# Attention steps 255 to 414 of a two-layer kernel: fixed strings of 16 steps, more double runs of values, five score tiles copied out by VectorE, ten tiles of exponentials

## The chip, the core and the metric

One core of a Trainium2 chip runs the whole program. TensorE multiplies (PE in the profile; its weight loads are PEld), VectorE is DVE, ScalarE ACT, GpSimd POOL, and SyncE (SP) issues most of the loads. Compute engines work on SBUF; TensorE writes its results to PSUM, which has eight banks of 512 float32 a partition. Each engine takes its instructions strictly in order and waits on semaphores for what the others make. The metric is the device time of one execution in microseconds.

## The reference

Four residual layers follow each other: attention, a Fourier mixing, attention, Fourier mixing. This is cut to the attention, which the change touches (S = 2048 tokens, D = 640, H = 32 heads of Dh = 20):

```python
qkv = (x @ wqkv).reshape(B, S, 3, H, Dh).transpose(2, 0, 3, 1, 4)
q, k, v = qkv[0], qkv[1], qkv[2]
scores = jnp.einsum("bhqd,bhkd->bhqk", q, k) * (Dh ** -0.5)
p = softmax(scores, axis=-1)
o = jnp.einsum("bhqk,bhkd->bhqd", p, v)
return o.transpose(0, 2, 1, 3).reshape(B, S, D) @ wo
```

## The kernel before

The 32 heads are taken in 8 groups of four, the queries in 4 blocks of 512, the keys in 16 blocks of 128. A **step** is one triple of them, in that order, so that a layer has 8 x 4 x 16 = 512 steps, and 16 steps in a row share one accumulator. A step makes two **score tiles** of 128 keys x (2 heads x 512 queries): `scores(n, j)` (line 606) issues two matmuls into a PSUM tile `psc` of two banks and one exponential on ScalarE (line 616) that reads `psc` and writes a tile `e` in SBUF. There are three `psc` tiles, taken in turn (six banks), and seven `e` tiles. `values(n)` (line 618) multiplies both `e` tiles of a step with the value matrix into the accumulator `acc` (one bank; line 624: four matmuls in the program, which the chip's records show as eight). One bank is left (`fill`).

After the 16th step of a head group's block, `finish` (line 629) copies `acc` away by a transpose on VectorE (line 631), normalizes it in six more VectorE instructions (lines 633 to 641) and sends eight DMAs from GpSimd's queue (line 645). The next step's values need `acc` free, so they wait for that transpose alone.

Three kinds of other work are laid between the steps. **Fills** are pieces of the projections for later heads: five matmuls of `pqk` (line 106) into the `fill` bank. After three pieces VectorE takes the product from the bank (`keep`, lines 91, 94, 262 to 267), and a **norm** follows (`norms`, line 283: one matmul, and a VectorE reduction at line 284). **Compares** are VectorE work on tables that GpSimd loads, to test that the Fourier matrices have the expected symmetry (pairs of lines 918 and 914, and smaller ones); `compare(n)` issues up to two of them a step. **Bounds** (lines 528 to 540) are small VectorE instructions with one power on GpSimd (line 536) between their head (528 to 530) and their tail (538, 540).

The order is that of the code, in `sweep` (line 648): each engine gets its instructions in the order in which Python issues them. In steps 255 to 414 no written string rules before the change: each step makes two score tiles, then a fill where `due` says so (three in 16 steps), or else one or two steps of values. This gives, on TensorE, two score tiles, then values of one step (a single run) or two (a double run), and so on. Strings written out by letters (`plan`, line 748) rule parts of the steps before 236 and those from 448.

Of the kernel before, what the change touches and what calls it, by code (L numbers as in the profile page):

```python
# [5 lines left out]
F32 = mybir.dt.float32  # L6
# [3 lines left out]
AF = mybir.ActivationFunctionType  # L10
# [6 lines left out]
SCALE = DH ** -0.5  # L17
# [25 lines left out]
def mha_fnet_kernel(ctx, tc, x_in, wqk, wv, wo, seq, hid, nat_seq, nat_hid, out):  # L43
    nc = tc.nc
    V, A, G, PE = nc.vector, nc.scalar, nc.gpsimd, nc.tensor
# [100 lines left out]
    class Qkv:  # L146
# [29 lines left out]
        def norm(s, k, tiles=range(2)):  # L176
            for i in tiles:
                normed(s.xn[k][:, i], s.xn[k][:, i], s.rs[k], i)
# [369 lines left out]

    class Attention:
        THIN = 236  # L550

        def __init__(s, qkv, L):
            s.a = qkv
            s.k, s.q, s.e = {}, {}, {}
            s.o = dr.tile([2, D, S], F32, name=f"o_{L}")
            s.steps = [(g, qb, kc) for g in range(H // 4) for qb in range(NB) for kc in range(NT)]

# [46 lines left out]
            G.memset(z[:H].bitcast(F32), 0.0)  # L604
            nc.sync.dma_start(s.a.shift["b"][:, 1], z[:H].bitcast(F32))

        def scores(s, n, j):

            g, qb, kc = s.steps[n]
            p = bank(f"p{(2 * n + j) % 3}", [128, 2, 512], "psc")  # L610
            for i in range(2):
                r = slice(64 * i, 64 * i + 62)
                PE.matmul(p[:, i], s.k[g, kc // 8, j][r, kc % 8 * 128:(kc % 8 + 1) * 128], s.q[g, qb, j][r],  # L613
                          start=True, stop=True)
            e = s.e[n, j] = s.room(f"e{(2 * n + j) % 7}", [2, 512], F32, "e")
            A.activation(e, p, AF.Exp, scale=SCALE)  # L616

        def values(s, n):
            g, qb, kc = s.steps[n]
# [9 lines left out]
        def finish(s, g, qb):  # L629
            t0 = s.room("ofsh", [16, 32], F32, "of")  # L630
            V.transpose(t0.rearrange("p b c -> p (b c)"), s.acc)  # L631
            rc = const.tile([128, 16], F32, name="rc", bufs=2)
            V.tensor_scalar(rc, t0[:, :, DH], 1e-30, None, op0=OP.max)
            V.reciprocal(rc, rc)
            t1 = s.room("on", [16, 32], F32, "on")
            V.tensor_tensor(t1, t0, rc[:, :, None].to_broadcast([128, 16, 32]), op=OP.mult)
            t2 = s.room("ofsh", [512], F32, "ot")
            V.transpose(t2, t1.rearrange("p b c -> p (b c)"))
            hl = [s.room("on", [512], F32R, "oh").bitcast(F32), t2]
            V.tensor_copy(hl[0].bitcast(F32R), t2)  # L640
            V.tensor_tensor(t2, t2, hl[0], op=OP.subtract)
            for k in range(2):
                for j in range(4):
                    h = 4 * g + j
                    G.dma_start(s.o[k, h * DH:(h + 1) * DH, qb * 512:(qb + 1) * 512],  # L645
                                hl[k][32 * j:32 * j + DH])

        def sweep(s, shift, begin, fill=lambda n: None, plan=None, block=None, compare=lambda n: None):
            done = calm = n = 0

            def opened(n):
                g, qb, kc = s.steps[n]
                begin(n, g, qb, kc)
                last = qb == NB - 1
                if kc == (7 if last else 10 if g in LATE else 4) and not (last and g == H // 4 - 1):
                    s.qload(*((g, qb + 1) if not last else (g + 1, 0)), shift)
                if last and g + 1 < H // 4:
                    for f, j in {1: [(0, 0)], 9: [(0, 1)], 11: [(1, 0)]}.get(kc, []):
                        s.kload(g + 1, f, j)
                if qb == 0 and kc == 0 and g:  # L660
                    s.kload(g, 1, 1)

            while n < len(s.steps):
                opened(n)
                order = plan and plan(n)
                if order:

                    while done < n - 1:
                        s.values(done)
                        done += 1  # L670
                    t = 2 * n
                    for c in order:
                        if c == "s":
                            m, j = divmod(t, 2)
                            if not j and m > n:
                                opened(m)
                            s.scores(m, j)
                            if j:
                                compare(m)
                            t += 1  # L680
                        elif c == "v":
                            s.values(done)
                            done += 1
                        else:
                            (block if c == "f" else fill)(t // 2)
                    n = t // 2
                    continue
                s.scores(n, 0)
                s.scores(n, 1)
                more, owed = fill(n) and n >= 2 and n + 1 < len(s.steps), n - 1 - done  # L690
                compare(n)
                n += 1
                if plan and n <= s.THIN:
                    count = owed + 1
                elif more and owed < 3:
                    calm = n + 1
                    continue
                else:
                    count = min(owed, 1)
                    if owed > 1 and (done + 1) % NT and n > calm:  # L700
                        calm = n + 1
                        count = 2
                for _ in range(count):
                    s.values(done)
                    done += 1
            for n in range(done, len(s.steps)):
                s.values(n)

        def run(s, done, project, check):

            work, tasks, later = s.a.work(), s.a.vweights(1, s.a.fill, pause=[lambda: None] * 2), list(check)
# [3 lines left out]
            tail, n = {}, 448  # L715
# [22 lines left out]
            def fill(n):  # L738
# [4 lines left out]
                elif s.work and n >= max(s.rest, s.THIN) and due(n + 1):  # L743
                    block(n)
                    s.rest = max(s.rest, n + 2)
                    return s.work and not s.a.silent

            def plan(n):
                if n in tail:
                    return tail[n]  # L750
                if s.blocks >= 58 or s.after:
                    return
                whole = 32 <= s.blocks < 48
                if n % 4 == 1 and n + (4 if whole else 8) < s.THIN and (whole or s.blocks % 2 == 0):
                    return "sssfsssvvssvv" if whole else "sssfsssvvssvvsssfssvvsssnvv"

            def compare(n):


                if n < 8:  # L760
                    return
                for _ in range(2):
                    if not later or n < s.landed or (len(check) - len(later)) * 490 >= n * len(check):
                        break
                    task = later.pop(0)
                    if isinstance(task, tuple):
                        s.landed = n + 5
                        task = task[1]
                    task()
# [8 lines left out]
            def begin(n, g, qb, kc):  # L778


                if qb == NB - 1 and g + 1 < H // 4:
                    when, to = 0, g + 1
                    c0, c1 = to * 80 // 128, ((to + 1) * 80 - 1) // 128
                    keys = [c0, (c1, 0) if to in LATE else c1, ND + c0, ND + c1] + (["v"] if to >= 4 else [])
                else:
                    when, to, keys = 5, g, [(((g + 1) * 80 - 1) // 128, qb + 1)]
                if to != g or g in LATE and qb < NB - 1:
                    if kc == when:
                        need(n, *keys)
                        s.shift = s.a.bound(to, s.room)  # L790
                    if kc - when in (0, 3, 5):
                        next(s.shift)

                if tasks and n % 2 == 0 and n >= 16 and n % 64 < 54:
                    tasks.pop(0)()
                for f in project.early.get(n, []):
                    f()

            s.sweep("b", begin, fill, plan, block, compare)
            assert not s.work and not later and not tasks and not project.parts, (len(later), len(tasks))  # L800

        def general(s, done, project):
# [252 lines left out]
    class Project:  # L1055
# [100 lines left out]
        @staticmethod  # L1156
        def scaled(dst, g, r, b2, b):

            A.activation(dst[:, :HD + 1], g[:, :HD + 1], AF.Identity, scale=r, bias=b2)
            A.activation(dst[:, 0:HD + 1:HD], g[:, 0:HD + 1:HD], AF.Identity, scale=r, bias=b)  # L1160
            A.activation(dst[:, HD + 1:], g[:, HD + 1:], AF.Identity, scale=r, bias=zero[:dst.shape[0]])
# [393 lines left out]
    tasks = check.tasks()  # L1555
    cut = next(i for i, t in enumerate(tasks) if 2 * i >= len(tasks) and isinstance(t, tuple))
    tasks = (tasks[:cut], tasks[cut:])
# [202 lines left out]
```

## Time and profile before

| | |
|---|---|
| three runs | 2429.83 us median (2429.36 to 2431.03) |
| the profiled execution | 2429.18 us, its span 2427.4 us |
| granted TensorE clock, mean | 0.998 |
| exponentials, line 616 | x2048, 1918.1 us busy, 1060 ns of one |
| value matmuls, line 624 | x8192, 1030.0 us busy |
| score matmuls, line 613 | x4096, 744.0 us busy |

A row of a group reads: line, engine, operation, output<-input by the program's names, partitions x elements, count, then busy time, mean of one, and the idle time of that engine before it with what ended it. A row of the timeline reads: start and length in us, engine, line, operation, output<-input, count of instructions merged; in square brackets the engine's idle time before, and what ended it. Matmuls overlap, so their run's cost is read from the start of one run to the start of the next. A row of the windows gives, for a stretch, busy time (and instructions) of PE, PEld, DVE, ACT and POOL in this order, then the granted clock, the share of the DMA engines and GB/s. The first layer's steps 255 to 414 lie between about 611 and 914.5 us, the second layer's between about 1815 and 2119 us.

### The profile page before, as it was taken

Reading aid. Unit: us, or ns where it says so; the run is one execution under the profiler, and the core shown is the slowest. Engines: PE = TensorE matmul, PEld = TensorE weight load, DVE = VectorE, ACT = ScalarE, POOL = GpSimd, SP = SyncE. Lnnn points to the kernel's source line nnn. Section 1 sums busy time; section 2 is a strip of 40 time slices with the busy share of each in tenths; the row PEclk is TensorE's granted clock in tenths of the full one; section 3 lists DMA queues with packets and bytes.
Section 4 is the critical chain, followed back from the end, with each engine's and each line's share of the span. In section 5 each row is a group of like instructions: output and inputs, shape, how many; then the busy total and the mean of one; then the engine's idle time right before and its main releaser. Section 6 shows DMA issues by size and latency. Waiting matters only on the chain. (4 is left out here: it accounts for less than half of the span.)

```text
span 2427.4 us, 43836 instructions
## 1 busy us (share of the span) xinstructions
PE 2406.3 (99%) x16200; PEld 1155.5 (48%) x16200; DVE 1012.3 (42%) x2328; ACT 2099.7 (86%) x2402; POOL 552.3 (23%) x1080
## 2 busy tenths in 40 slices
PE   9999999999999999999999999999999999999998
PEld 8544444543333332339885444454433333333496
DVE  7333432234333434427773444332433333334275
ACT  5799998899999999994357999988999999999852
POOL 3122221012222212114341212211111212113143
PEclk9999999999999999999999999999999999999999
DMA  6334341123232325419663232322231322152195
GB/s 213 130 122 137 110 150 59 60 69 119 80 93 89 105 72 159 124 48 320 238 230 116 96 118 89 116 65 77 77 109 57 96 59 81 52 154 78 53 333 211
DMA packets 136702, 289.01 MB, mean 119 GB/s; under 512 B 31628, under 2 KB 56108, under 8 KB 136480
## 3 DMA queue, kind: packets, MB, share of 16 engines
q1 hardware_dynamic: 93408, 171.07, 21.7%
q0 software_dynamic: 43072, 115.06, 14.8%
q8 instruction: 130, 2.13, 0.4%
q14 instruction: 92, 0.75, 0.1%
HBM read 187.38 MB, written 92.70 MB: 115 GB/s over the span
## 5 line engine op out<-in xcount | busy, mean ns | idle before, releaser
L616 ACT ACTIVATE e<-psc 128x1024 f32<-128x1024 f32 x2048 | 1918.1, 1060 | 106.5 <-PE psc L613 96.4
L624 PE MATMUL acc<-e,v 128*32 128x512 f32 x8192 | 1030.0, 600 | 0.4 <-DVE of L631 0.4
L613 PE MATMUL psc<-stq,stk 62*128 62x512 f32 x4096 | 744.0, 446 | 3.1 <-ACT e L616 2.2
L613 PEld LDWEIGHTS psc<-stq,stk 62*128 62x128 f32 x4096 | 335.0, 184 | 699.9 <-ACT e L616 545.5
L624 PEld LDWEIGHTS acc<-e,v 128*32 128x32 f32 x8192 | 210.7, 109 | 410.0 <-issue 378.0
L106 PE MATMUL pqk<-xt,wqk 128*128 128x512 f32 x1200 | 320.9, 408 | 2.1 <-ACT xt L93 1.1
L645 POOL DMA_DIRECT2D o<-oh x256 | 131.6, 522 | 784.6 <-DVE oh L640 737.0
L91 DVE CAST hl<-pqk 128x512 fp32r<-128x512 f32 x64 | 44.3, 692 | 587.7 <-PE pqk L106 587.7
L106 PEld LDWEIGHTS pqk<-xt,wqk 128*128 128x128 f32 x1200 | 214.2, 189 | 86.1 <-issue 38.4
L106 PE MATMUL pv<-wv,xt 128*128 128x320 f32 x960 | 151.7, 314 | 0.0
L106 PEld LDWEIGHTS pv<-wv,xt 128*128 128x128 f32 x960 | 141.0, 188 | 13.5 <-issue 10.2
L631 DVE STREAM_TRANSPOSE of<-acc 128x512 f32<-128x512 f32 x64 | 45.8, 715 | 208.7 <-PE acc L624 208.7
L645 POOL DMA_DIRECT2D o<-ot x256 | 128.2, 508 | 1.8 <-DVE xr L1118 0.6
L275 POOL DMA_DIRECT2D scrk<-hl x40 | 27.9, 697 | 377.4 <-DVE hl L94 266.6
L275 POOL DMA_DIRECT2D scrq<-hl x40 | 28.4, 711 | 352.8 <-DVE hl L94 293.2
L99 PE MATMUL py<-wo,o 128*128 128x320 f32 x320 | 101.2, 316 | 0.0
L914 DVE TENSOR_REDUCE far<-cq 128x1 f32<-128x512 f32 (+5 forms) x169 | 98.5, 584 | 5.7
L101 PE MATMUL py<-wo,o 128*128 128x320 f32 x320 | 98.9, 309 | 0.0
L100 PE MATMUL py<-wo,o 128*128 128x320 f32 x320 | 98.8, 309 | 0.0
L918 DVE TENSOR_TENSOR cq<-cq 128x512 f32<-128x512 f32 (+4 forms) x166 | 96.5, 581 | 1.2 <-DMA cq<-in_nat_seq_dram 1.2
L314 DVE COPY v<-pv 128x320 f32<-128x320 f32 x32 | 15.7, 489 | 161.8 <-PE pv L106 161.8
L284 DVE TENSOR_REDUCE top<-pn 32x1 f32<-32x512 f32 x50 | 33.7, 676 | 72.3 <-PE pn L283 72.2
(219 smaller groups left out, 1744.5 us busy)
## 6 DMA issues: line engine op xcount, KB each, us to landing
cq<-in_nat_seq_dram POOLq DMA_DIRECT2D x64, 512.0 KB, 5.3
scrq<-hl POOLq DMA_DIRECT2D x40, 512.0 KB, 4.1
scrk<-hl POOLq DMA_DIRECT2D x40, 512.0 KB, 3.2
stq<-scrq SPq DMA_DIRECT2D x256, 80.0 KB
stk<-scrk SPq DMA_DIRECT2D x128, 160.0 KB
chl<-matrix SPq DMA_DIRECT2D x32, 512.0 KB
o<-o SPq DMA_DIRECT2D x32, 384.0 KB
stq<-scrq SPq DMA_DIRECT2D x256, 40.0 KB
```

What stands on the lines that cost most here:

```text
L99: PE.matmul(out_ap, ah, bh, start=start, stop=False)
L100: PE.matmul(out_ap, ah, bl, start=False, stop=False)
L101: PE.matmul(out_ap, al, bh, start=False, stop=stop)
L106: yield lambda i=i, j=j, k=k: PE.matmul(out_ap, a[i], b[j], start=dc == 0 and k == 0, stop=dc == ND - 1 and k == 2)
L275: G.dma_start(s.scr["qk"[k]][c * 128:(c + 1) * 128, :, tb * 512:(tb + 1) * 512], hl.bitcast(F32))
L613: PE.matmul(p[:, i], s.k[g, kc // 8, j][r, kc % 8 * 128:(kc % 8 + 1) * 128], s.q[g, qb, j][r], start=True, stop=True)
L616: A.activation(e, p, AF.Exp, scale=SCALE)
L624: PE.matmul(s.acc[32 * j:32 * j + 32], s.a.v[kc][:, v0:v0 + 32], s.e[n, j // 2][:, j % 2], start=kc == 0, stop=kc == NT - 1, skip_group_ch ...
L631: V.transpose(t0.rearrange("p b c -> p (b c)"), s.acc)
L645: G.dma_start(s.o[k, h * DH:(h + 1) * DH, qb * 512:(qb + 1) * 512], hl[k][32 * j:32 * j + DH])
L914: V.tensor_reduce(to, x, op=OP.max, axis=AX.X, apply_absolute_value=True)
L918: V.tensor_tensor(y, x, y, op=op)
```

## The change

Steps 255 to 414 (ten strings of 16 in each layer) follow one written string. Its letters: `s` a score tile with its exponential out of PSUM; `d` a score tile that VectorE first copies from `psc` to its `e` tile, after which the exponential works in place in SBUF; `v` the values of the oldest step that has none yet; `f` a fill; `n` the norm, if one is pending. Two more tiles of score lead over values are let in (`done < n - 2`).

Between the value runs, the string is: `ss f s v`, `ss v` four times, `sd f ssd vv`, `ssd vv`, `ssd f ss vv`, `ss v n`, `ss vv`, `ssd vv`, and one `s` that joins the next string's first two. Its first value is that of the 15th step of a group's 16, so that its third `v` closes a group and its fourth opens the next.

Three more `e` tiles come from the space of a weight tile that is no longer used (`widen`), and are given back after step 414 (`narrow`). The part of `finish` behind the transpose, the compares, and the tasks that load later weights are no longer issued where they arise, but put into `held`; `release` issues them after the letter at hand, unless one of the next two letters is a `d`. This holds in all steps, with and without a string.

```diff
     class Attention:
         THIN = 236
+        LOOSE = range(255, 415, 16)
+        STRING = "ssfsvssvssvssvssvsdfssdvvssdvvssdfssvvssvnssvvssdvvs"
...
+            s.ring = [lambda k=k: s.room(f"e{k}", [2, 512], F32, "e") for k in range(7)]
...
-        def scores(s, n, j):
+        def scores(s, n, j, copied=False):
...
-            e = s.e[n, j] = s.room(f"e{(2 * n + j) % 7}", [2, 512], F32, "e")
-            A.activation(e, p, AF.Exp, scale=SCALE)
+            s.ring.append(s.ring.pop(0))
+            e = s.e[n, j] = s.ring[-1]()
+            if copied:
+                V.tensor_copy(e, p)
+            A.activation(e, e if copied else p, AF.Exp, scale=SCALE)
+
+        def widen(s):
+            x = s.a.fill("wv", [3, 2, 512], F32, "ex")
+            s.extra = [lambda k=k: x[:, k] for k in range(3)]
+            s.ring = s.extra + s.ring
+
+        def narrow(s):
+            s.ring = [f for f in s.ring if f not in s.extra]
...
             V.transpose(t0.rearrange("p b c -> p (b c)"), s.acc)
+            s.held.append(lambda: s.scaled(t0, g, qb))
+
+        def scaled(s, t0, g, qb):
             rc = const.tile([128, 16], F32, name="rc", bufs=2)
...
+            def release():
+                while s.held:
+                    s.held.pop(0)()
...
-                    while done < n - 1:
+                    while done < n - (2 if n in s.LOOSE else 1):
                         s.values(done)
                         done += 1
+                    if n in s.LOOSE and done == n - 1:
+                        order = order.replace("v", "", 1)
                     t = 2 * n
-                    for c in order:
-                        if c == "s":
+                    for k, c in enumerate(order):
+                        if c in "sd":
...
-                            s.scores(m, j)
+                            s.scores(m, j, c == "d")
                             if j:
-                                compare(m)
+                                s.held.append(lambda m=m: compare(m))
...
-                            (block if c == "f" else fill)(t // 2)
+                            (block if c == "f" else fill if n < s.THIN else norm)(t // 2)
+                        if k + 1 < len(order) and "d" not in order[k + 1:k + 3]:
+                            release()
...
+                release()
                 s.scores(n, 0)
...
+            def norm(n):
+                if s.after:
+                    f, s.after = s.after[1], None
+                    f()
...
+                if n in s.LOOSE:
+                    if n == s.LOOSE[0]:
+                        s.widen()
+                    return s.STRING
+                if n == s.LOOSE[-1] + 16:
+                    s.narrow()
...
-                    tasks.pop(0)()
+                    s.held.append(tasks.pop(0))
```

What this moves is seen in the program's order, engine by engine. First TensorE, in the first layer, around steps 306 to 312 (`psc` scores, `acc` values, `pqk` a fill; `ex` are the three new exponential tiles; values of one step are four rows here). Before:

```order
L613 MATMUL psc<-stq,stk 128x512 x4
L106 MATMUL pqk<-xt,wqk 128x512 x5
L613 MATMUL psc<-stq,stk 128x512 x4
L624 MATMUL acc<-e,v 32x512 x4
L613 MATMUL psc<-stq,stk 128x512 x4
L624 MATMUL acc<-e,v 32x512 x8
L613 MATMUL psc<-stq,stk 128x512 x4
L624 MATMUL acc<-e,v 32x512 x4
```

And now, from the run that ends in the string's first copied tile:

```order
L616 MATMUL psc<-stq,stk 128x512 x4
L106 MATMUL pqk<-xt,wqk 128x512 x5
L616 MATMUL psc<-stq,stk 128x512 x6
L638 MATMUL acc<-ex,v 32x512 x2
L638 MATMUL acc<-e,v 32x512 x6
L616 MATMUL psc<-stq,stk 128x512 x6
L638 MATMUL acc<-e,v 32x512 x8
```

Score tiles now come three at a time (x6) where two steps of values follow (eight rows), instead of two at a time with mostly one step of values.

Second, VectorE in the same place, from the transpose that frees the accumulator on. Before:

```order
L631 STREAM_TRANSPOSE of<-acc 128x512
L633 TENSOR_SCALAR rc<-of 128x16
L634 RECIPROCAL rc<-rc 128x16
L636 TENSOR_TENSOR on<-of,rc 128x512
L638 STREAM_TRANSPOSE ot<-on 128x512
L640 CAST oh<-ot 128x512
L641 TENSOR_TENSOR ot<-ot,oh 128x512
L918 TENSOR_TENSOR cq<-cq 128x512
L914 TENSOR_REDUCE far<-cq 128x1
L538 TENSOR_SCALAR bound<-bound 32x1
L540 CAST sh<-bound 32x64
```

And now:

```order
L645 STREAM_TRANSPOSE of<-acc 128x512
L650 TENSOR_SCALAR rc<-of 128x16
L651 RECIPROCAL rc<-rc 128x16
L653 TENSOR_TENSOR on<-of,rc 128x512
L655 STREAM_TRANSPOSE ot<-on 128x512
L657 CAST oh<-ot 128x512
L658 TENSOR_TENSOR ot<-ot,oh 128x512
L956 TENSOR_TENSOR cq<-cq 128x512
L952 TENSOR_REDUCE far<-cq 128x1
L538 TENSOR_SCALAR bound<-bound 32x1
L540 CAST sh<-bound 32x64
L621 COPY e<-psc 128x1024
```

The sequence is the same, and the copy of the string's first `d` tile stands behind all of it. In the other strings the same seven instructions of the finish come first; between them and the copy stand, in the first layer's ten strings in order, a compare pair and the bound's head; the same; the head; pair and tail (the rows above); a maximum with eight small compare instructions; nothing; nothing; pair and tail; pair and head; a maximum and the head. In the second layer: the head; three small ones and the head; the head; tail and pair; a pair; nothing; a maximum with two small ones; the tail; the head; the head.

More of the change, by code (lines that the diff above doesn't have):

```diff
@@ L550, in mha_fnet_kernel @@
         THIN = 236
+        LOOSE = range(255, 415, 16)
+        STRING = "ssfsvssvssvssvssvsdfssdvvssdvvssdfssvvssvnssvvssdvvs"
         def __init__(s, qkv, L):
             s.a = qkv
-            s.k, s.q, s.e = {}, {}, {}
+            s.k, s.q, s.e, s.held = {}, {}, {}, []
+            s.ring = [lambda k=k: s.room(f"e{k}", [2, 512], F32, "e") for k in range(7)]
             s.o = dr.tile([2, D, S], F32, name=f"o_{L}")
@@ L646, in finish, with sweep @@
                                 hl[k][32 * j:32 * j + DH])
-        def sweep(s, shift, begin, fill=lambda n: None, plan=None, block=None, compare=lambda n: None):
+        def sweep(s, shift, begin, fill=lambda n: None, plan=None, block=None, compare=lambda n: None, norm=None):
             done = calm = n = 0
+            def release():
+                while s.held:
+                    s.held.pop(0)()
             def opened(n):
@@ L707, in sweep @@
                 s.values(n)
+            release()
         def run(s, done, project, check):
@@ L794, in begin @@
                 if tasks and n % 2 == 0 and n >= 16 and n % 64 < 54:
-                    tasks.pop(0)()
+                    s.held.append(tasks.pop(0))
                 for f in project.early.get(n, []):
                     f()
-            s.sweep("b", begin, fill, plan, block, compare)
+            s.sweep("b", begin, fill, plan, block, compare, norm)
             assert not s.work and not later and not tasks and not project.parts, (len(later), len(tasks))
```

## The prediction

> **What bounds the kernel now.** I read the page's busy shares first, then busy time by windows, then TensorE's timeline in the stretch that is changed (first layer; the second layer's rows look alike).
>
> ```profile
> PE 2406.3 (99%) x16200; PEld 1155.5 (48%) x16200; DVE 1012.3 (42%) x2328; ACT 2099.7 (86%) x2402; POOL 552.3 (23%) x1080
> ...
> core 0: us, PE busy (x) PEld busy (x) DVE busy (x) ACT busy (x) POOL busy (x), PEclk, DMA share, GB/s
> 611.00:914.50 303.50, 303.50 (x2080) 107.36 (x2076) 117.55 (x262) 299.46 (x320) 62.87 (x113) 1.00 0.28 88
> 914.50:943.40 28.90, 28.73 (x195) 8.54 (x194) 12.76 (x32) 28.90 (x33) 6.72 (x12) 1.00 0.37 110
> ```
>
> Steps 255 to 414 last 303.5 us for 160 steps: TensorE without a gap, ScalarE at 98.7%, granted clock 1.00, VectorE at 39%. Two engines are nearly full. One period of 16 steps on TensorE shows which is the tighter:
>
> ```profile
> 699.43 0.73 PE L613 MATMUL psc<-stq,stk 62*128 62x512 f32 x4
> 700.10 1.06 PE L624 MATMUL acc<-e,v 128*32 128x512 f32 x8
> 701.10 0.73 PE L613 MATMUL psc<-stq,stk 62*128 62x512 f32 x4
> ...
> 703.41 1.06 PE L624 MATMUL acc<-e,v 128*32 128x512 f32 x8
> 704.41 0.90 PE L613 MATMUL psc<-stq,stk 62*128 62x512 f32 x4
> 705.24 1.43 PE L106 MATMUL pqk<-xt,wqk 128*128 128x512 f32 x5
> 706.59 0.73 PE L613 MATMUL psc<-stq,stk 62*128 62x512 f32 x4
> ...
> 708.25 0.73 PE L613 MATMUL psc<-stq,stk 62*128 62x512 f32 x4
> 708.91 1.92 PE L624 MATMUL acc<-e,v 128*32 128x512 f32 x16
> 710.77 0.73 PE L613 MATMUL psc<-stq,stk 62*128 62x512 f32 x4
> ...
> 729.80 0.73 PE L613 MATMUL psc<-stq,stk 62*128 62x512 f32 x4
> ...
> 821.63 1.07 PE L624 MATMUL acc<-e,v 128*32 128x512 f32 x8
> 822.51 0.38 PE L283 MATMUL pn<-sq,ind 128*32 128x512 bf16 x1
> 822.82 0.73 PE L613 MATMUL psc<-stq,stk 62*128 62x512 f32 x4
> ```
>
> From start to next start: a score run of two tiles 0.66 (708.25 to 708.91), a run of values 1.00, a double run 1.86, a fill 1.35, a norm 0.19 more (821.63 to 822.82 is 1.19). Sixteen steps hold 16 score runs, 10 single and 3 double value runs, 3 fills and a norm: 10.56 + 10.0 + 5.58 + 4.05 + 0.19 = 30.4; the trace has 30.37 (699.43 to 729.80). So TensorE sets the pace. ScalarE's own floor stands where it never waits:
>
> ```profile
> 914.53 29.45 ACT L616 ACTIVATE e<-psc 128x1024 f32<-128x1024 f32 x32
> ...
> 973.52 1.02 ACT L616 ACTIVATE e<-psc 128x1024 f32<-128x1024 f32 x1 [0.21 <-PE psc L613]
> ```
>
> (29.45 - 1.02) / 31 = 0.917 a tile, 29.34 for a period. ScalarE idles 1.03 of 30.37.
>
> **What is removed.** The new string has 14 score runs and 11 value runs (6 single, 5 double) for the same 32 tiles, 16 steps, 3 fills and norm.
>
> ```profile
> 972.90 0.97 PE L613 MATMUL psc<-stq,stk 62*128 62x512 f32 x6
> ...
> 1066.22 0.97 PE L613 MATMUL psc<-stq,stk 62*128 62x512 f32 x6
> 1067.13 1.92 PE L624 MATMUL acc<-e,v 128*32 128x512 f32 x16
> ```
>
> Three tiles take 0.91, two 0.66: about 0.24 a tile and 0.18 a run. Scores: 14 x 0.18 + 32 x 0.24 = 10.20, 0.36 less. Values: 6 x 1.00 + 5 x 1.86 = 15.3, 0.28 less. TensorE alone would need 29.73. That is 0.39 over ScalarE's floor, so from here each wait of ScalarE counts.
>
> **What is late next.** A first score tile's exponential starts 0.62 after its run (972.90 to 973.52). ScalarE's stock is the work it has beyond what TensorE has just delivered; it idles where this runs out. A single run with two tiles takes 1.66 and brings 1.83 of ScalarE's work, +0.18. "ss vv" takes 2.52 for 1.83: -0.68. "sss vv" (2.76 for 2.75), the first piece and "ssvn" come out even; both pieces with a fill and a double (0.66 + 1.35 + 0.91 + 1.86 = 4.78 for five tiles, 4.59) lose 0.19. The stock is zero at the first of the four "ssv", grows to 0.70, and loses 0.28 at the border of a head group: there the old string put a fill between the last values of one group and the first of the next, now only two score tiles stand there. Let the last values start at T. VectorE's transpose of the accumulator starts at T + 1.14 (703.41 to 704.55, below), which is 0.08 after the values end (704.47); I take that 0.08 for every signal from engine to engine. It ends at T + 1.86, so TensorE, back at T + 1.66, goes on at T + 1.94: 0.28. The remaining 0.42 goes into the pieces with fills, and the later "ss vv" finds none: ScalarE idles 0.68 there, about 0.12 a little before (TensorE itself waits for score buffers in the second piece with a fill), and 0.16 at the first copied tile (next part). 29.34 + 0.96 = 30.30 a string, 0.07 under 30.37: 1.4 us for 20 strings is all that is left of 20 x 0.64.
>
> **The copies.** No row copies 128x1024 out of PSUM; the nearest are
>
> ```profile
> L91 DVE CAST hl<-pqk 128x512 fp32r<-128x512 f32 x64 | 44.3, 692 | 587.7 <-PE pqk L106 587.7
> ...
> L640 DVE CAST oh<-ot 128x512 fp32r<-128x512 f32 x64 | 27.3, 427 | 2.2
> ...
> L314 DVE COPY v<-pv 128x320 f32<-128x320 f32 x32 | 15.7, 489 | 161.8 <-PE pv L106 161.8
> ```
>
> 1.06 ns an element between the two PSUM rows (pqk and pv) gives 1.23 us. Bounds: two casts out of PSUM, 1.38, and two out of SBUF, 0.85. I take 1.23, the line through the PSUM rows. When may the first of the five begin? In program order it stands behind the whole finish of the head group:
>
> ```profile
> 704.55 0.72 DVE L631 STREAM_TRANSPOSE of<-acc 128x512 f32<-128x512 f32 x1 [4.99 <-PE acc L624]
> ...
> 707.73 0.69 DVE L641 TENSOR_TENSOR ot<-ot,oh 128x512 f32<-128x512 f32 x1
> 708.34 0.68 DVE L918 TENSOR_TENSOR cq<-cq 128x512 f32<-128x512 f32 x1
> 709.06 0.69 DVE L914 TENSOR_REDUCE far<-cq 128x1 f32<-128x512 f32 x1
> 709.66 0.13 DVE L538 TENSOR_SCALAR bound<-bound 32x1 f32<-32x1 f32 x1
> 709.83 0.25 DVE L540 CAST sh<-bound 32x64 fp32r<-32x64 f32 x1
> 709.94 0.67 DVE L918 TENSOR_TENSOR cq<-cq 128x512 f32<-128x512 f32 x1
> ...
> 823.65 0.18 DVE L528 TENSOR_REDUCE boundm<-top 32x10 f32<-32x40 f32 x1
> ...
> 824.05 0.15 DVE L530 TENSOR_TENSOR bound<-bound 32x1 f32<-32x1 f32 x1
> ```
>
> The finish takes 704.55 to 708.34, 3.79, so VectorE is free at T + 1.14 + 3.79 = T + 4.93. The tile is there at T + 1.00 + 0.66 + 0.28 + 1.00 + 0.66 + 1.00 (its run starts, T + 4.60) + 0.73 + 0.08 = T + 5.41, so 0.48 is spare. ScalarE wants it at T + 4.60 + 0.62 + 0.42 of stock + 0.92 for the tile before it = T + 6.56; copied at once it comes at 5.41 + 1.23 + 0.08 = T + 6.72. So VectorE work beyond the spare 0.48 is ScalarE's idle time, one for one. TensorE cannot work ahead meanwhile: three score buffers block it. The change holds VectorE work back only when a copy is one or two letters away, and these items are issued earlier. Extra work ahead of the first copy, by the new program order: a compare pair (1.32, 708.34 to 709.66) and the bound's head (about 0.5, 823.65 to past 824.05), late by 1.34: 3 strings; the pair and the bound's tail (0.28), 1.12: 3; the pair alone, 0.84: 1; other compare work, which I estimate at 0.6 late, between none and the longest: 4; head or tail alone, within the spare time: 6; nothing: 3. Sum 4.0 + 3.4 + 0.8 + 2.4 = 10.6 us. The other four copies have VectorE free, or 0.5 to spare on ScalarE.
>
> Exponentials now read SBUF five times a string.
>
> ```profile
> L93 ACT ACTIVATE xt<-xs 128x512 fp32r<-128x512 f32 x20 | 10.8, 618 | 3.4 <-DMA scrk<-hl 3.2 <-DMA stk<-scrk 0.2
> ...
> L93 ACT ACTIVATE xt<-ptr 128x512 fp32r<-128x512 f32 x20 | 10.2, 605 | 0.7 <-PE ptr L187 0.7
> ```
>
> The same copy costs 13 ns more from SBUF: 100 exponentials, 1.3 us. The Trainium skill ("VectorE: DVE Perf Modes", section "The TRN2 errata — SBUF-src ops pay a fixed extra latency per instruction") has 224 fixed cycles for ScalarE from SBUF and 172 from PSUM at 1.2 GHz, a rule against this change; by it an estimate of 43 ns each, 4.3 us, and a time 3 us higher. The rows' 13 ns speak for less.
>
> **At no cost.** Ten exponential tiles in place of seven only remove waits. Holding the finish and the compares elsewhere moves VectorE work by a step: before step 255 TensorE has no gap, after 414 VectorE is busy 12.76 of 28.90. Were that cover gone, only the transpose could be waited for, and it isn't held.
>
> **The sum.** The profiled execution took 2429.18 (span 2427.4; median 2429.83): - 1.4 + 10.6 + 1.3 gives 2439.7.
>
> **Rivals.** (1) *VectorE is in time*: the compare items wait elsewhere, or TensorE reaches the first copied tile over a microsecond later than I count. Strings of 30.30, - 1.4 + 1.3: 2429.1, no change. For it: VectorE is idle 61% of the stretch. Against: the finish and the pair stand in one row ahead of the copy. (2) *Faster*: ScalarE holds one more tile (0.92) at the first copied tile, the point from which it decides; the delays then vanish and so do its idle spells, and TensorE's 29.73 + 0.28 rules. 20 x 0.36 less: 2422.0. For it: ten exponential tiles and early-freed buffers let TensorE lead. Against: three score buffers bound the lead, and only tiles already copied are free of that. (3) *Worse*: the bound's tail on VectorE waits for GpSimd's power, which stands behind eight output DMAs of 0.52 (4.1 us), issued after the finish; they end about T + 9, and the third copy is wanted at T + 10.2. If the finish slips by 1.5 it costs up to 1 us in eight strings: 2447.7. That the change does not do what it says is ruled out by the program order, which has the runs and the copies.
>
> ```profile
> L645 POOL DMA_DIRECT2D o<-oh x256 | 131.6, 522 | 784.6 <-DVE oh L640 737.0 <-DVE ot L641 46.1 <-issue 1.6
> ```
>
> **How the numbers follow.** Late first copies, with (3) as its far end: 0.62. VectorE in time: 0.24. Faster: 0.14. The likeliest gives 2439.7, between 2433 and 2449: a copy of 0.85 takes off 0.38 in 11 late strings and the 0.16 in nine others, 5.6 in all, one of 1.38 adds 20 x 0.15, and (3) adds 8. To hold 8 in 10 the range takes in rival (1) and ends at 2425. A measurement tells 0.2% (4.9 us) from no change, so faster 0.14, same 0.24, slower 0.62.
>
> **What would show it.** In the profile after: a score run of three tiles near 0.9 and 29.73 of TensorE work in a string if nothing waits; the copy near 1.23; the first copy of a string starting later than its tile by the listed delays, with ScalarE idle before its exponential on VectorE; strings of 31.1 to 31.7 with a pair and near 30.3 without. Strings all near 30.3 make (1) right; near 30.0, (2); VectorE held by GpSimd's power ahead of the third copy, (3). The forecast is wrong if VectorE waits nowhere ahead of the first copy.

## The result and the profile after

| | before | after |
|---|---|---|
| median of the runs, us | 2429.81 (2428.71 to 2431.03, six runs) | 2441.99 (2440.36 to 2444.03, six runs) |
| profiled execution, us | 2429.18 | 2442.70 |
| its span, us | 2427.4 | 2440.9 |
| steps 255 to 414, first and second layer, us | 303.51, 303.93 | 312.27, 307.86 |

After over before is 1.0051, 95% interval 1.0041 to 1.0062: 12 us slower. The granted clock is 0.998 in both profiles. Here and below a stretch of steps runs from the end of the last exponential ahead of it to the end of its own last one.

First the page of the changed kernel, to be set beside the busy shares of before (engine, busy time, share of the span, instructions):

```profile
PE 2407.5 (99%) x16200; PEld 1158.8 (47%) x16200; DVE 1131.7 (46%) x2428; ACT 2096.0 (86%) x2402; POOL 551.3 (23%) x1080
...
L621 DVE COPY e<-psc 128x1024 f32<-128x1024 f32 x68 | 83.2, 1223 | 82.2 <-PE psc L616 81.0
```

VectorE has 100 copies more, 68 into `e` tiles (the row) and 32 into `ex`, 1.223 us each (1.23 was foretold). TensorE still stands at 99% of the whole span, but the busy times of the changed stretch say otherwise. The rows of before, one for each layer:

```profile
609.08:912.59 303.51, 303.51 (x2076) 107.51 (x2068) 117.55 (x262) 299.59 (x321) 62.87 (x113) 1.00 0.29 89
1812.94:2116.87 303.93, 303.93 (x2076) 107.59 (x2068) 102.07 (x253) 300.07 (x320) 61.08 (x113) 1.00 0.24 70
```

And of after:

```profile
608.98:921.25 312.27, 305.75 (x2085) 109.49 (x2083) 178.63 (x317) 298.12 (x321) 63.01 (x113) 1.00 0.29 88
1822.41:2130.27 307.86, 303.46 (x2085) 109.60 (x2083) 163.62 (x310) 298.14 (x322) 60.99 (x113) 1.00 0.24 71
```

TensorE was busy for all of both stretches before, and ScalarE idle for 3.9 us of each. Now TensorE is idle for 6.5 and 4.4 us, and ScalarE for 14.2 and 9.7. What ended ScalarE's idle time shows in its groups for the exponentials that read SBUF:

```profile
L622 ACT ACTIVATE e<-e 128x1024 f32<-128x1024 f32 x68 | 72.8, 1071 | 6.2 <-DVE e L621 5.8
L622 ACT ACTIVATE ex<-ex 128x1024 f32<-128x1024 f32 x32 | 34.2, 1068 | 2.9 <-DVE ex L621 2.6
```

So ScalarE stands 9.1 us before copied tiles, 8.4 of them for VectorE's copy. The worst case is the string that begins at step 383; this is VectorE's timeline there (start, duration, instruction):

```profile
863.71 0.72 DVE L645 STREAM_TRANSPOSE of<-acc 128x512 f32<-128x512 f32 x1 [3.38 <-PE acc L638]
...
866.89 0.69 DVE L658 TENSOR_TENSOR ot<-ot,oh 128x512 f32<-128x512 f32 x1
867.50 0.68 DVE L956 TENSOR_TENSOR cq<-cq 128x512 f32<-128x512 f32 x1
868.22 0.69 DVE L952 TENSOR_REDUCE far<-cq 128x1 f32<-128x512 f32 x1
868.82 0.17 DVE L528 TENSOR_REDUCE boundm<-top 32x10 f32<-32x40 f32 x1
...
869.21 0.15 DVE L530 TENSOR_TENSOR bound<-bound 32x1 f32<-32x1 f32 x1
869.29 1.23 DVE L621 COPY e<-psc 128x1024 f32<-128x1024 f32 x1
```

VectorE has no gap from the transpose to the copy: finish, a compare pair, the bound's head, and only then the tile, 1.33 us after TensorE had written it. ScalarE in the same string:

```profile
864.51 4.73 ACT L622 ACTIVATE e<-psc 128x1024 f32<-128x1024 f32 x5
870.55 1.06 ACT L622 ACTIVATE e<-e 128x1024 f32<-128x1024 f32 x1 [1.31 <-DVE e L621]
...
881.92 2.87 ACT L622 ACTIVATE ex<-psc 128x1024 f32<-128x1024 f32 x3 [0.18 <-PE psc L616]
...
886.30 1.94 ACT L622 ACTIVATE e<-psc 128x1024 f32<-128x1024 f32 x2 [0.59 <-PE psc L616]
```

And TensorE there:

```profile
869.24 0.73 PE L616 MATMUL psc<-stq,stk 62*128 62x512 f32 x4
870.57 0.51 PE L616 MATMUL psc<-stq,stk 62*128 62x512 f32 x2 [0.59 <-DVE e L621]
...
876.92 1.42 PE L106 MATMUL pqk<-xt,wqk 128*128 128x512 f32 x5
878.27 0.50 PE L616 MATMUL psc<-stq,stk 62*128 62x512 f32 x2
879.03 0.51 PE L616 MATMUL psc<-stq,stk 62*128 62x512 f32 x2 [0.25 <-ACT e L622]
```

Two different losses stand here. At 870.55 ScalarE waits for the late copy, and TensorE behind it for the buffer that this copy frees. At 881.92 (tile 24, counted from 0 in the string) and 886.30 (tile 28) ScalarE waits for TensorE, which had itself waited at 879.03: behind the third fill the second score tile finds all three buffers taken.

From here on, what ScalarE idles at a tile is counted as in the prediction: the time from the end of the exponential ahead to the end of the tile's own, less the 0.917 us that one takes back to back. The brackets of the timeline stop at the start of the exponential and show 0.11 to 0.14 less (1.31 above is 1.45 here).

Counted over the twenty strings: in nine the first copy starts 0.11 us after its tile, as soon as it can, ScalarE idles 0.22 to 0.24 there, and the string takes 30.41 to 30.95 us. In eleven it starts 0.20 to 1.33 us after it, ScalarE idles the same amount longer (0.80 late: 0.92 idle; 1.15: 1.24; 1.33: 1.45), and the string takes 30.72 to 31.90. What ScalarE idles over 0.23 at that tile sums to 7.4 us. Of the 13.5 us of span, 12.7 lie in steps 255 to 414, 1.5 in steps 448 to 511 of the two layers, and steps 415 to 447 give 0.5 back. The 1.5 is one late transpose in each layer. VectorE after:

```profile
985.04 0.48 DVE L91 CAST wo<-woraw 128x640 fp32r<-128x640 f32 x1
985.56 0.83 DVE L94 TENSOR_TENSOR wo<-woraw,wo 128x640 fp32r<-128x640 f32 x1
986.30 0.71 DVE L645 STREAM_TRANSPOSE of<-acc 128x512 f32<-128x512 f32 x1
```

The split of a weight (lines 91 and 94), one of the items that are now held and released, has come ahead of the accumulator's transpose. Before, it came after the finish:

```profile
977.10 0.72 DVE L631 STREAM_TRANSPOSE of<-acc 128x512 f32<-128x512 f32 x1 [0.41 <-PE acc L624]
...
980.90 0.49 DVE L91 CAST wo<-woraw 128x640 fp32r<-128x640 f32 x1
```

TensorE waits some 0.8 us for the accumulator at that border.

### The profile page after: what moved, and what is told of

It reads as the page before. It is cut to its first block, busy times and chain, and to the rows that moved or that the text cites. A ratio compares the mean times of both kernels' runs of the same rounds, so it can differ in the third digit from the quotient of the medians.

```text
span 2440.9 us, 43936 instructions
## 1 busy us (share of the span) xinstructions
PE 2407.5 (99%) x16200; PEld 1158.8 (47%) x16200; DVE 1131.7 (46%) x2428; ACT 2096.0 (86%) x2402; POOL 551.3 (23%) x1080
## 5 line engine op out<-in xcount | busy, mean ns | idle before, releaser
L622 ACT ACTIVATE e<-psc 128x1024 f32<-128x1024 f32 x1788 | 1683.5, 1064 | 108.9 <-PE psc L616 106.6
L638 PE MATMUL acc<-e,v 128*32 128x512 f32 x7424 | 958.4, 600 | 3.6 <-DVE of L645 3.6
L638 PEld LDWEIGHTS acc<-e,v 128*32 128x32 f32 x7424 | 200.0, 108 | 371.2 <-issue 335.0
L622 ACT ACTIVATE ex<-psc 128x1024 f32<-128x1024 f32 x160 | 156.7, 1049 | 5.6 <-PE psc L616 5.6
L106 PEld LDWEIGHTS pv<-wv,xt 128*128 128x128 f32 x960 | 141.0, 188 | 13.5 <-issue 10.2
L638 PE MATMUL acc<-ex,v 128*32 128x512 f32 x768 | 130.9, 601 | 1.2 <-DVE of L645 1.2
L621 DVE COPY e<-psc 128x1024 f32<-128x1024 f32 x68 | 83.2, 1223 | 82.2 <-PE psc L616 81.0
```

Source lines behind the costliest of these rows:

```text
L106: yield lambda i=i, j=j, k=k: PE.matmul(out_ap, a[i], b[j], start=dc == 0 and k == 0, stop=dc == ND - 1 and k == 2)
L621: V.tensor_copy(e, p)
L622: A.activation(e, e if copied else p, AF.Exp, scale=SCALE)
L638: PE.matmul(s.acc[32 * j:32 * j + 32], s.a.v[kc][:, v0:v0 + 32], s.e[n, j // 2][:, j % 2], start=kc == 0, stop=kc == NT - 1, skip_group_ch ...
```

## The experiments

Ratios are against the kernel before on the same chip, with 95% intervals. "Stretch" is the sum of steps 255 to 414 of both layers in the one profiled execution: 607.44 us before, 620.13 after. Steps 16 to 254, which no run's string touches, take 493.5 to 493.8 us a layer in all thirteen profiles, so a few tenths between two stretches mean nothing.

**1. The order of before, all else as changed.**

```
-                    return s.STRING
+                    pass
```

> Steps 255 to 414 go back to the order of before; the ten exponential tiles and the held finishes and compares of the change stay. Theory (the string and its copies make the whole difference): strings of 30.37 us again, 2429.8 within 1 us. Rival (the other edits cost: held work, ten tiles, moved buffers): part of the 12 us stays, 2432 or more.

2428.22 us, ratio 0.9998 (0.9989 to 1.0007). Its stretches:

```profile
608.05:911.71 303.66, 303.66 (x2076) 107.16 (x2068) 117.55 (x262) 296.41 (x320) 62.87 (x113) 1.00 0.29 89
1811.25:2114.95 303.70, 303.70 (x2074) 107.12 (x2068) 102.48 (x254) 296.40 (x320) 61.08 (x113) 1.00 0.24 71
```

TensorE is without a gap again. Held work and ten exponential tiles cost nothing and bring nothing by themselves, in the stretch and in steps 448 to 511 alike: the string with its copies makes the difference.

**2. The string without its copies.**

```
-        STRING = "ssfsvssvssvssvssvsdfssdvvssdvvssdfssvvssvnssvvssdvvs"
+        STRING = "ssfsvssvssvssvssvssfsssvvsssvvsssfssvvssvnssvvsssvvs"
```

> The string stays with its long runs, but all five copied tiles are read by ScalarE straight from PSUM. Theory (the change loses by first copies that start late, 7.4 us, and by dearer exponentials; the later copies are worth about 0.2 us a string, since without them TensorE meets a full set of score buffers earlier): strings all alike at about 30.6 us, none of 31 and more; about 8.6 us less than the changed kernel, 2433.4. Rival A (the copies carry the string, their lateness costs nothing): slower than 2442. Rival B (VectorE's queue is not what costs): 2442 as before, with strings still uneven.

2442.72 us, ratio 1.0061 (1.0048 to 1.0075), stretch 622.00. The strings are alike, but take 30.95 to 31.19, not 30.6. ScalarE in one of them:

```profile
797.77 4.69 ACT L622 ACTIVATE e<-psc 128x1024 f32<-128x1024 f32 x5 [0.23 <-PE psc L616]
...
809.98 1.94 ACT L622 ACTIVATE e<-psc 128x1024 f32<-128x1024 f32 x2 [0.19 <-PE psc L616]
...
817.80 3.79 ACT L622 ACTIVATE e<-psc 128x1024 f32<-128x1024 f32 x4 [0.38 <-PE psc L616]
822.17 2.85 ACT L622 ACTIVATE ex<-psc 128x1024 f32<-128x1024 f32 x3 [0.59 <-PE psc L616]
```

ScalarE waits at four places, all for TensorE, which is held by the score buffers. So the long runs alone lose, and the copies are worth more than was expected, by some 0.5 us a string. The time, just over 2442, is the one that rival A foretold: the copies carry the string. The other half of rival A, that their lateness costs nothing, is left to run 4.

**3. Only the first copy taken back.**

```
-        STRING = "ssfsvssvssvssvssvsdfssdvvssdvvssdfssvvssvnssvvssdvvs"
+        STRING = "ssfsvssvssvssvssvssfssdvvssdvvssdfssvvssvnssvvssdvvs"
```

> Only the first of the five copied tiles of a string goes back to a direct exponential; the other four stay copied. Theory (the first copy stands behind the finish and the compares and is the only one that ScalarE waits for): every string about 30.37 us, about 12 us less than the changed kernel, 2429.9, no better than before since ScalarE's idle time before the tile 24 and the tile 28 stays. Rival A (the other four copies are late as well): strings stay uneven, 2435 or more. Rival B (the first copy is worth something when it is in time): strings of 30.6 and more.

2436.03 us, ratio 1.0033 (1.0021 to 1.0045), stretch 613.94. No string is long for a late copy; most take 30.47 to 30.73, four 30.96 to 31.04. ScalarE's 0.23 now stands before the second copied tile. So the late first copy is gone, but the strings do not come down to the 30.37 expected, and the time is in the rivals' range. Rival A's late copies did not come; rival B, that a first copy in time is worth something, is left to run 4. The first copy was not what kept the strings with a copy in time at 30.4 to 30.9.

**4. All copies, the compares and the bound after the first.**

```
...
-            s.held.append(lambda: s.scaled(t0, g, qb))
+            s.first.append(lambda: s.scaled(t0, g, qb))
...
-            def release():
-                while s.held:
-                    s.held.pop(0)()
+            def release(keep=False):
+                while s.first or s.held and not keep:
+                    (s.first or s.held).pop(0)()
...
-                            release()
+                            release(n in s.LOOSE and done > n and k < order.index("d"))
...
-                        next(s.shift)
+                        s.held.append(lambda: next(s.shift)) if 255 <= n < 415 and n % 16 in (3, 5) else next(s.shift)
```

> All five copies stay; between the finish of a head group and the first copy of a string VectorE gets no compares and no items of the bound, which are issued right after the first copy. Theory (extra VectorE work ahead of the first copy is ScalarE's idle time one for one): the first copy starts within 0.15 us of its tile in all 20 strings, a second copy is late by about 0.8 in a few, within its 0.5 us of spare but for 0.3; strings between 30.2 and 30.8, about 8.9 us less than the changed kernel, 2433. By the prediction's own sum for the late copies it would be 10.6 less, 2431.4. Rival (the wait only moves to the second copy, or lateness is harmless): 2440 to 2442, with ScalarE's idle time now before the second copied tile.

The first copy starts 0.11 us after its tile in all twenty strings. Idle ahead of the exponentials that read SBUF:

```profile
L622 ACT ACTIVATE e<-e 128x1024 f32<-128x1024 f32 x68 | 72.7, 1069 | 1.1
L622 ACT ACTIVATE ex<-ex 128x1024 f32<-128x1024 f32 x32 | 34.2, 1068 | 0.7
```

9.1 us has become 1.8, and the stretch is 613.14, 7.0 less than in the changed kernel, where 8.9 was expected. Second copies are late by up to 0.8, which costs 0.14 to 0.19 us in three strings, where 0.3 was expected. The median is 2437.2, ratio 1.0036 (1.0022 to 1.005): by the two ratios the gain is 3.6 us, but their intervals are 3.4 us to each side here and 2.5 for the changed kernel, which leaves room for 7.0. The profiled execution lost 1.5 us in the first 16 steps of the second layer, which the edit does not touch. Lateness is thus worth 7.0 us here; 5.7 us over the stretch of before stay with no copy late.

Set beside the run without copies, this gives the worth of the copies: 622.00 - 613.14 = 8.9 us, of which the changed kernel gave 7.0 back by lateness. And beside run 3: 613.94 - 613.14 is 0.04 us a string, so the first copy, the one that causes the lateness, brings next to nothing even in time.

**5. The third fill one tile earlier.**

```
-        STRING = "ssfsvssvssvssvssvsdfssdvvssdvvssdfssvvssvnssvvssdvvs"
+        STRING = "ssfsvssvssvssvssvsdfssdvvssdvvsdfsssvvssvnssvvssdvvs"
```

> Only one place of the string moves: the third fill is issued before the last tile of its run of three, ssdfssvv becomes sdfsssvv, so that TensorE no longer stands before a score buffer behind that fill (1.18 us in place of 0.66 for its two-tile run). Theory (ScalarE's idle 0.27 at tile 24 and most of the 0.69 at tile 28 come from this one wait): the two spells shrink to none and about 0.25, strings without a late copy about 30.05 us, the lateness of the first copies stays; 20 x 0.6 = 12 us less than the changed kernel, 2430. Rival (the idle spells come from the two tiles before the double run, wherever the fill stands): strings of 30.5 and more, 2440.

The copied tile ahead of that fill moves with it, from tile 21 to 20.

2431.83 us, ratio 1.0014 (1.0004 to 1.0023), stretch 611.45, 8.7 less, of the 12 expected. TensorE behind the third fill:

```profile
872.62 1.43 PE L106 MATMUL pqk<-xt,wqk 128*128 128x512 f32 x5
873.98 0.96 PE L616 MATMUL psc<-stq,stk 62*128 62x512 f32 x6
874.88 1.48 PE L638 MATMUL acc<-ex,v 128*32 128x512 f32 x10
```

Three tiles follow the fill and none waits. The idle spell at tile 24 is gone and that at tile 28 is 0.33 in place of 0.69; a new one of 0.20 stands at the copied tile 20. Strings with the first copy in time take 30.12 to 30.17, apart from the first of a layer and two with a spell of their own. Late copies remain as they were. One wait for a score buffer had been worth some 0.44 us a string, at two places of ScalarE. What the copied tile's move gives of this was not run by itself.

**6. Another string, its copies far behind the border.** It has the same parts, and four copies.

```
+        STRING = "ssvsvssvssfssvssvssvvssdfssdvvsssvvsdfssdvvsssvvssvn"
```

> Another string of the same parts (32 tiles, 16 steps of values, three fills, a norm) with four copied tiles, the first of them fifteen tiles behind the border of the head group, fills only before a tile whose score buffer is free, double runs only where ScalarE has stock. Theory (hand walk of the string with the durations of the traces: every piece even, ScalarE idle 0.3): strings of 29.8 to 29.9 us, no late copy over 0.5, about 22 us less than the changed kernel and 10 less than before, 2419.5. Rival (VectorE's other work makes copies late here too, or ScalarE needs more than 29.5): strings of 30.4 and more, no better than before.

2436.36 us, ratio 1.0032 (1.0019 to 1.0044), stretch 615.16, strings of 30.36 to 31.99 where 29.8 to 29.9 was expected: the rival. VectorE before the fourth copy:

```profile
817.22 1.23 DVE L621 COPY e<-psc 128x1024 f32<-128x1024 f32 x1 [4.09 <-PE psc L616]
818.51 0.69 DVE L91 CAST hl<-pqk 128x512 fp32r<-128x512 f32 x1
819.24 0.69 DVE L94 TENSOR_TENSOR hl<-pqk,hl 128x512 fp32r<-128x512 f32 x1
819.84 0.68 DVE L262 TENSOR_TENSOR sq<-hl 128x512 bf16<-128x512 f32 x1
820.44 1.22 DVE L621 COPY e<-psc 128x1024 f32<-128x1024 f32 x1
```

The third fill ends a block of the projection. VectorE's three instructions on that block (six in six of the strings) stand in its row ahead of the fourth copy, which starts 1.07 to 2.67 us after its tile in all twenty. The expectation had left out what a fill puts on VectorE.

**7. A string without copies.**

```
+        STRING = "ssvssfssvssvssfssvssvvsssvvssfsssvvssvsnssvvsssvvssv"
```

> A string of the same parts without any copied tile. Theory (copies are not needed where no fill stands behind a run that fills all three score buffers): TensorE sets the pace at 30.0 to 30.1 us a string, all strings alike; 2424, 6 us less than before. Rival (without copies a double run always costs ScalarE an idle spell, as in the run without copies, 31.15): 30.6 or more a string, 2434 or more.

2426.25 us, ratio 0.9991 (0.9981 to 1.0000), stretch 605.59. The strings are alike at 30.24 to 30.32, 0.1 under those of before, and ScalarE idles 0.90 to 0.98 in each: between the two expectations, and hardly to be told from no change. A string without any copy is thus level with before, and 14.5 us better in the stretch than the changed one.

**8. The string of run 6, its tiles uncopied.**

```
+        STRING = "ssvsvssvssfssvssvssvvsssfsssvvsssvvssfsssvvsssvvssvn"
```

> The string of the run with four later copies, its copied tiles read straight from PSUM. Theory: TensorE waits 0.7 us for a score buffer at the first of them and 0.2 at another, strings of 30.7 us, 2438: there the copies are worth 0.9 us a string. Rival (the order alone makes the gain): strings under 30.1, 2424.

2436.26 us, ratio 1.0034 (1.0021 to 1.0047), stretch 614.82; strings of 30.48 to 30.90, as expected. With its copies that string took 615.16: in it, too, the late copy takes back what the others are worth.

**9. Both repairs together.** The fill of run 5 and the held compares of run 4.

> Both repairs of the changed string together: the third fill one tile earlier and the compares and the bound's items after the first copy. Theory (the two costs are separate and add up): strings of 30.12 us as those without a late copy in the run with the fill alone, against 30.37 to 30.46 before; 20 x 0.27 = 5.4 us less than before, a ratio of 0.998. Rival (with TensorE further ahead the second copy becomes the late one): strings of 30.4 and more, no better than before.

2424.48 us, ratio 0.9981 (0.9972 to 0.9990), as expected, and faster than both kernels, if by 0.2% against before. Its stretches:

```profile
608.58:910.99 302.41, 300.76 (x2085) 110.97 (x2083) 178.37 (x317) 298.24 (x322) 63.05 (x113) 1.00 0.31 93
1811.21:2113.44 302.23, 300.62 (x2085) 110.98 (x2083) 164.12 (x310) 298.19 (x322) 60.99 (x113) 1.00 0.26 74
```

604.64 in all, 15.5 less than the changed kernel; the two repairs alone gave 7.0 and 8.7. They add up: two separate costs. The stretch is only 1.0 under that of run 7, which has no copy at all.

**10 and 11. Two strings with the copies behind the third block's work on VectorE.**

```
+        STRING = "svsfssvssvssvssfssvssvssvvsssfssvvssdvvssdvvssdnvvss"
```

> A string of the same parts with three copied tiles, all behind the third fill's VectorE work (the run with four later copies showed a copy that stands 2.3 us behind the third fill late by 1.07 to 2.67 us, since it waits in VectorE's row behind the end of that fill's block). Theory: no copy late, ScalarE idle 0.5, strings of 29.9 to 30.1 us, 8 us less than before, a ratio of 0.997. Rival (some other VectorE item stands ahead of a copy): uneven strings, 30.4 or more.

2424.98 us, ratio 0.9986 (0.9977 to 0.9995), stretch 604.33. That is less than half of the 8 us expected, by the stretch, and half by the median. Most strings take 29.98 to 30.15, but the first of each layer takes 30.9; in two others a compare ahead of the first copy still costs 0.46 and 0.50.

```
+        STRING = "sdvvsssvsfssvssvssfssvssvsvssfsssvvssdvvssdvvnssdvvs"
```

> As the string before, but with a fourth copied tile as the second tile of the string, ahead of the head group's last values, and the fills elsewhere. Theory: no copy late, ScalarE idle 0.4, strings of 29.9 to 30.0 us, 9 us less than before, a ratio of 0.996. Rival: as for the string before; by the copy at the string's start a late one would show as ScalarE's idle time before tile 1.

2426.40 us, ratio 0.9990 (0.9981 to 0.9999), stretch 605.43. Of the 9 us expected 2.0 come in the stretch and 2.7 in the median. Twelve of its strings take 29.82 to 30.04, the shortest of them shorter than any other run's. But four are longer by 0.8 to 1.9, where a weight's split and the norm's reduction stand ahead of the last copy, as the rival had it.

## Why the prediction was right, and where its sizes were off

**Late first copies, + 10.6.** The mechanism and the place were right: VectorE's row ahead of the first copy, beyond its spare time, is ScalarE's idle time one for one. Eleven late strings were foretold, and those eleven came. The size was 7.4 by ScalarE's idle time and 7.0 by the run that took the lateness away. A copy in time starts 0.11 after its tile, so that 0.11 comes off each delay before it is set beside the forecast: a compare pair and the bound's head cost 1.22 at step 383 (1.34 foretold), and pair and tail 1.04 and 1.03 in two strings (1.12 foretold). At steps 255 and 271 the compared blocks are 256 wide, not 512, and pair and head cost 0.69; in the second layer a pair with the tail and a pair alone are some 320 wide and cost 0.62 and 0.35. I had priced every pair by one row of the full width, and that is the larger part of the 3.2 us too much.

**The string without VectorE's delay, 30.30.** This was the weak term. In run 4, where no first copy is late, the stretch is 5.7 us above before, not the 0.1 below that - 1.4 and + 1.3 make. ScalarE's large idle spells stand at the three foretold tiles, but in a string with a norm they are 0.23, 0.27 and 0.69 where I had 0.16, 0.12 and 0.68, and in the six without one they sum to 1.01. Over twenty strings that is 3.5 us more. The first string of each layer also idles 0.35 at tile 3, which the walk did not have: 0.7 us in all. TensorE's own work was counted well: where nothing waits, three score tiles take 0.90 from start to next start (run 5, 873.98 to 874.88; 0.91 was foretold), and the shortest string of all, 29.82 in run 11, which has the same parts, comes near the 29.73 foretold for TensorE alone.

The worse error was to take the 0.68 as given by the two tiles before the double run. Run 5 shows that half of it, with the 0.27, goes when TensorE no longer waits behind the third fill. I had named that wait, and put it at 0.12.

**Exponentials from SBUF, + 1.3.** From the end of one exponential to the end of the next, back to back, it is 0.946 us where the tile is in SBUF and 0.917 where it is in PSUM; after an idle time one takes 1.058 against 1.025 (medians). That is 0.03 each, 3 us for the hundred, so the 13 ns from the 512-wide copies were too little. The estimate of 43 ns from the Trainium skill ("VectorE: DVE Perf Modes", "The TRN2 errata — SBUF-src ops pay a fixed extra latency per instruction") is 13 ns too much here, with the right sign.

Not all of the 3 us comes on top, since the first copied tile's share stands in its 0.23 already: the others make 2.2 in run 4, 0.9 more than the term. Run 4 also has spells in single strings, 0.3 at tile 28 of step 335, 0.3 at tile 31 of step 383 in the second layer, and 0.5 at three late second copies. - 0.1 + 3.5 + 0.7 + 0.9 + 1.1 is 6.1 for the 5.7 measured; the rest is that exponentials from PSUM often follow each other in 0.915, not 0.917.

**The sum.** It came within 2.3 us of the median by luck: the string was 5.8 us dearer than foretold, the late copies 3.6 us cheaper, and the 1.5 us of the late transposes, less 0.5, stood in no term.

**The copy, 1.23.** It took 1.223 us, on the line through the two rows out of PSUM.

**At no cost.** Ten exponential tiles and held work cost nothing with the old order (run 1). But I left the transpose out of the held work's reach too soon: it isn't held itself, yet a released weight split stands ahead of it once in each layer, 1.5 us together. Runs 2, 3, 4, 6 and 8 have this too, and runs 1, 5, 7, 9, 10 and 11 do not, though their work is held as well: it hangs on the string, by a way that was not followed up.

**The rivals.** VectorE in time: eleven strings say no, and run 4 shows that even then the changed string would not have been level with before. Faster by a tile more of stock: no string came near 30.0 (the shortest is 30.41); TensorE stood before the three score buffers (870.57 and 879.03 above), as said against it. GpSimd's power: the third copy stood behind the bound's tail and was late by 0.31 and 0.36 in two strings, and ScalarE did not idle there; this costs nothing.

Still open: which strings bring a weight's split ahead of a transpose, what the copied tile's move in run 5 gives by itself, and what an exponential from SBUF costs at other widths than 1024.

## What to carry to other kernels

Where two engines are both nearly full, handing a step of one to a third engine that is mostly idle helps only if that engine gets to the step in the time that the next one has to spare: read, in program order, all that stands ahead of it, also what another engine's work (here a fill) will put there. And before trading runs for fewer, longer ones, walk the buffers: one tile that waits behind a long fill cost the engine behind it twice, at two later places, and moving the fill by one tile was worth more (8.7 us) than what the late copies lost (7.0). Try a string without copies as well: run 7, without any copy, came within 1.3 us of the best stretch with copies.

## What was not expected of the hardware

An exponential of 128x1024 costs 0.03 us more from SBUF than from PSUM, where a copy of 128x512 on the same engine cost 0.013 more. And handing over is not equally quick between engines: ScalarE's exponential starts 0.034 us after VectorE's copy ends, while VectorE's copy starts 0.11 after the records have the tile's last matmul end; I had taken 0.08 for both.
